# Loading a KV cache in 2 MiB pieces instead of 1 MiB pieces in a decode kernel, with a reshaped query weight, a later output weight and a bf16 GELU

## The chip, the cores and the metric

The kernel runs on one core of one Trainium2 chip. The metric is the device time of one execution in microseconds (us), as the median of several executions. All executions quoted are fast: on one core none was more than 1.5% above the fastest of its kernel.

## The reference

One decode step. A single token attends to a long cache, a small token-mixer MLP runs on the same token, and a sigmoid gate mixes the two.

```python
# x (1,1,448); k_cache, v_cache (1,8,65536,256) bf16; wq (448,4096); wo (4096,448)
def reference(A_x, A_k_cache, A_v_cache, A_wq, A_wo, B_x, B_w1, B_b1, B_w2, B_b2, gate_w):
    # ... attention: 16 query heads, 8 key-value heads, head size 256
    q = (x @ wq) per head
    scores = einsum("bhqd,bhkd->bhqk", q, k) * 256 ** -0.5
    o = einsum("bhqk,bhkd->bhqd", softmax(scores), v)
    a = o @ wo
    # ... mixer: layernorm, u = gelu(h * w1 + b1) with F = 1792, y = w2 . u + b2
    return g * a + (1 - g) * b          # g = sigmoid(sum(x * gate_w))
```

The caches hold 2 x 8 x 65,536 x 256 bf16 elements, which is 537 MB. The two attention weights add 7.3 MB. Every byte is read once, so this is a streaming problem.

## The kernel before

The cache is cut into 256 chunks of 2,048 keys: 1 MiB of K and 1 MiB of V each, 8 KiB on each of 128 partitions. For each chunk TensorE transposes K (32 matmuls against an identity), VectorE and ScalarE copy the result out of PSUM, TensorE makes the scores (32 matmuls), ScalarE takes the exponential, and TensorE multiplies by V (32 matmuls) and sums the denominators (1). SyncE issues all loads from one queue, in the order written, and it waits for a free slot before it issues into it.

```python
    KB = 3          # K slots of 1 MiB
    VB = 4          # V slots of 1 MiB
    # ...
            # SyncE: small rows first, then the query weight, 448 rows as 4 x 112 partitions
            eng.dma_start(wq_sb[:, :, :], A_wq.rearrange("(kt c) n -> c kt n", c=KCP)).then_inc(sem_wq, 16)

            def k_dma(c):
                g, k = divmod(c, NCPH)
                slot = c % KB
                if c >= KB:
                    eng.wait_ge(sem_tr, NB * (c - KB + 1))        # the slot's transposes are done
                src = A_k_cache[0, g, k * CH:(k + 1) * CH, :].rearrange("(p n) d -> p (n d)", p=P)
                eng.dma_start(kbuf[:, slot, :, :].rearrange("p n d -> p (n d)"), src).then_inc(sem_k[slot], 16)
            # ... v_dma(c) likewise, waiting for sem_pv

            WO_AT = min(4, NC - 1)
            for c in range(NC + 2):
                if c < NC:
                    k_dma(c)
                cv = c - 2
                if 0 <= cv < NC:
                    v_dma(cv)
                if c == WO_AT:
                    eng.dma_start(wo_sb[:, :, :], A_wo.rearrange("(kt p) n -> p kt n", p=P)).then_inc(sem_wo, 16)
    # ...
            # TensorE, after the last chunk
            pe.wait_ge(s_rden, 1)
            # ... one matmul spreads the reciprocal denominators
            for kt in range(FT):                                   # 14 matmuls: second MLP layer
                ins = pe.matmul(sps[0:1, 0, 0:DM], w2p_b[:, kt:kt + 1], gu[:, kt, :],
                                start=(kt == 0), stop=(kt == FT - 1))
            # ... 32 matmuls: output projection with wo_sb
```

The softmax here doesn't subtract the row's maximum and nothing guards it: scores larger than these inputs give would overflow.

## Time and profile before

| | before |
|---|---|
| median, 13 executions | 1358.16 us (1357.3 to 1359.97) |
| bytes moved | 547.7 MB |
| TensorE (PE) busy | 87% |
| DMA busy from slice 2 to slice 39 of 40 | 90% or more |
| rate from 100 to 1300 us | 412 to 416 GB/s |

The lines below are from the profile page of the kernel before: the span; the engines with their busy time; the span in 40 slices, where a digit of the DMA row is the busy share in tenths and the row below is GB/s; the packet counts; the queue that fetches instructions (packets, MB, share); the chain of work that ended last; one group of instructions (name, shapes, count | busy us, mean ns | idle us before it, and what ended it); and one DMA issue (count, size, us from issue to landing).

```profile
span 1357.0 us, 53691 instructions
...
PE 1177.8 (87%) x25056; PEld 1143.9 (84%) x25056; DVE 403.1 (30%) x623; ACT 547.8 (40%) x787; POOL 1.0 (0%) x9
...
DMA  8999999999999999999999999999999999999994
GB/s 277 395 418 419 419 419 415 407 418 412 416 413 409 420 408 412 413 419 412 414 411 416 411 410 419 412 411 419 408 409 414 410 416 417 408 415 411 415 411 166
DMA packets 78538, 547.69 MB, mean 404 GB/s; under 512 B 8232, under 2 KB 12331, under 8 KB 12334
...
q8 instruction: 199, 3.26, 1.0%
...
DMA kbuf<-in_A_k_cache_dram 64%; PE kst L258 25%; PE po L291 3%; PE sps L274 3%; DMA wq_sb<-in_A_wq_dram 1%; DMA vbuf<-in_A_v_cache_dram 1%; PE sps L318 0%; SPq L174 0%; PE den L295 0%; PE sps L305 0%; PE sps L237 0%; SPq L182 0%; DVE out_f L427 0%; DVE diff L425 0%; PE den L300 0%
...
L258 PE MATMUL kst<-ident,kbuf 128*128 128x128 bf16 x8192 | 720.0, 268 | 131.9 <-DMA kbuf<-in_A_k_cache_dram 130.0
...
wq_sb<-in_A_wq_dram SPq DMA_DIRECT2D x1, 3584.0 KB, 18.0
```

The DMA row stands at 9 in all slices but the first and the last, while PE is 87% busy. The first slice is slow (277 GB/s), since the query weight is loaded there, and the second has a dip (395). The chain names K loads for 64% of the span. The largest group on PE, the transposes, idled 131.9 us, of which waits for K ended 130.0. PE can keep up; it waits for data.

The next lines are the stretch table of the kernel before: time range and length, busy time of each engine, granted PE clock, DMA share and rate.

```profile
core 0: us, PE busy (x) PEld busy (x) DVE busy (x) ACT busy (x) POOL busy (x), PEclk, DMA share, GB/s
100.00:300.00 200.00, 175.26 (x3850) 171.46 (x3849) 65.03 (x101) 84.89 (x124) 0.00 (x0) 0.78 1.01 416
...
900.00:1100.00 200.00, 179.01 (x3812) 175.32 (x3809) 54.89 (x80) 82.42 (x118) 0.00 (x0) 0.76 1.01 412
```

A DMA share of 1.01 means that the 16 DMA engines had a packet in hand practically all the time (the records of consecutive packets overlap by some 4 ns, so the share can pass 1). When the engines are always busy, the time is in the packets themselves. So the second reading is of single packets, from the trace's records ("at best" is the time that 99% of the packets reach or exceed):

```
packets of the kernel before    count    ns, at best   ns, mean
8,192 B  (K, V, query weight)  65,984     309          318.8
896 B    (output weight)        4,096      41           46
4 B      (semaphore)            8,231       9            9
16,384 B (instruction block)      199     940        1,061
line through 896 B and 8,192 B:  8 ns + 0.0367 ns per byte, which is 27.2 GB/s for each engine, 435 for 16
```

The fixed 8 ns is what a larger packet saves. The 435 GB/s is the line worked out for 16 engines, an estimate from these two packet sizes. Over the 1,200 us from 100 to 1300 us this one core took 412 to 416 GB/s from HBM.

### The profile page before, as it was taken

How to read it: one execution, taken by the hardware profiler on the slowest of the kernel's cores; microseconds unless marked ns; L12 is line 12 of the kernel's file. 1: busy time of each engine (PE TensorE's matmuls, PEld its weight loads, DVE VectorE, ACT ScalarE, POOL GpSimd, SP SyncE). 2: the span in 40 equal slices, each digit the busy share in tenths (PEclk: the TensorE clock that was granted, in tenths of full speed). 3: DMA queues.
4: the chain of work that ended last, by engine and by line, in shares of the span. 5: the costliest groups of instructions: out<-in, count | busy, mean ns of one | idle time of the engine just before them, and what ended most of it. 6: DMA issues, size and time to landing. Idle time of an engine off the chain costs nothing.

```text
span 1357.0 us, 53691 instructions
## 1 busy us (share of the span) xinstructions
PE 1177.8 (87%) x25056; PEld 1143.9 (84%) x25056; DVE 403.1 (30%) x623; ACT 547.8 (40%) x787; POOL 1.0 (0%) x9
## 2 busy tenths in 40 slices
PE   4588889898899898898888888998898899899897
PEld 4588888788898898898888888888888899889885
DVE  2585222222222222222222222222222222222222
ACT  2354344344343443443443443434434344444341
POOL 0000000000000000000000000000000000000000
PEclk9778787788777877867887876877877867767768
DMA  8999999999999999999999999999999999999994
GB/s 277 395 418 419 419 419 415 407 418 412 416 413 409 420 408 412 413 419 412 414 411 416 411 410 419 412 411 419 408 409 414 410 416 417 408 415 411 415 411 166
DMA packets 78538, 547.69 MB, mean 404 GB/s; under 512 B 8232, under 2 KB 12331, under 8 KB 12334
## 3 DMA queue, kind: packets, MB, share of 16 engines
q1 hardware_dynamic: 78318, 544.26, 98.1%
q8 instruction: 199, 3.26, 1.0%
q14 instruction: 21, 0.17, 0.0%
HBM read 544.22 MB, written 0.00 MB: 401 GB/s over the span
## 4 chain that ended last, share of the span: by engine, by line
DMA 67%; PE 32%; issue 1%; SPq 1%; DVE 0%; DVEq 0%
DMA kbuf<-in_A_k_cache_dram 64%; PE kst L258 25%; PE po L291 3%; PE sps L274 3%; DMA wq_sb<-in_A_wq_dram 1%; DMA vbuf<-in_A_v_cache_dram 1%; PE sps L318 0%; SPq L174 0%; PE den L295 0%; PE sps L305 0%; PE sps L237 0%; SPq L182 0%; DVE out_f L427 0%; DVE diff L425 0%; PE den L300 0%
## 5 line engine op out<-in xcount | busy, mean ns | idle before, releaser
L258 PE MATMUL kst<-ident,kbuf 128*128 128x128 bf16 x8192 | 720.0, 268 | 131.9 <-DMA kbuf<-in_A_k_cache_dram 130.0
L455 ACT ACTIVATE ktT<-kst 128x1024 bf16<-128x1024 bf16 x512 | 513.4, 1022 | 781.4 <-PE kst L258 781.3
L258 PEld LDWEIGHTS kst<-ident,kbuf 128*128 128x128 bf16 x8192 | 666.2, 124 | 150.3 <-DMA kbuf<-in_A_k_cache_dram 145.2
L392 DVE COPY ktT<-kst 128x1024 bf16<-128x1024 bf16 x512 | 353.6, 691 | 912.1 <-PE kst L258 900.1
L291 PE MATMUL po<-pT,vbuf 128*128 128x2 bf16 x8192 | 247.6, 164 | 22.3 <-issue 18.5
L274 PE MATMUL sps<-qT,ktT 128*128 128x2 bf16 x8192 | 251.2, 164 | 3.5 <-issue 3.5
L274 PEld LDWEIGHTS sps<-qT,ktT 128*128 128x128 bf16 x8192 | 247.1, 100 | 4.1 <-issue 3.9
L291 PEld LDWEIGHTS po<-pT,vbuf 128*128 128x128 bf16 x8192 | 228.7, 97 | 24.0 <-issue 20.9
L461 ACT ACTIVATE pT<-sps 128x32 bf16<-128x32 f32 x255 | 50.2, 197 | 1.5 <-PE sps L274 1.3
L295 PE MATMUL den<-pT,ones_col 128*1 128x32 bf16 x256 | 46.0, 180 | 0.0
L295 PEld LDWEIGHTS den<-pT,ones_col 128*1 128x1 bf16 x256 | 20.3, 79 | 5.6 <-issue 0.9
L237 PEld LDWEIGHTS sps<-xcol,wq_sb 112*128 112x128 bf16 x128 | 3.5, 104 | 10.3 <-issue 10.3
L237 PE MATMUL sps<-xcol,wq_sb 112*128 112x1 bf16 x128 | 3.6, 165 | 9.0 <-DMA wq_sb<-in_A_wq_dram 9.0
L371 DVE TENSOR_TENSOR zring<-wring,uring 128x448 f32<-128x448 f32 x14 | 8.8, 626 | 1.2 <-issue 0.2
L366 DVE TENSOR_TENSOR wring<-uring 128x448 f32<-128x448 f32 x14 | 8.8, 626 | 1.1
L380 DVE TENSOR_TENSOR gu<-tring,uring 128x448 bf16<-128x448 f32 x14 | 8.8, 625 | 1.1
L443 ACT ACTIVATE tring<-zring 128x448 f32<-128x448 f32 x14 | 8.2, 583 | 0.0
L363 DVE TENSOR_SCALAR uring<-hbT,params 128x448 f32<-128x448 f32 x14 | 7.1, 507 | 0.0
L318 PE MATMUL sps<-wo_sb,oTn 128*1 128x448 bf16 x32 | 6.2, 352 | 0.0
L368 DVE TENSOR_SCALAR wring<-wring 128x448 f32<-128x448 f32 x14 | 5.5, 394 | 1.1
L227 PE MATMUL sps<-h_row,ones_row_f 1*128 1x448 f32 x2 | 1.9, 1026 | 4.5 <-DVE h_row L351 4.5
L318 PEld LDWEIGHTS sps<-wo_sb,oTn 128*1 128x1 bf16 x32 | 2.7, 84 | 3.4
(55 smaller groups left out, 31.0 us busy)
## 6 DMA issues: line engine op xcount, KB each, us to landing
kbuf<-in_A_k_cache_dram SPq DMA_DIRECT2D x256, 1024.0 KB, 12.4
vbuf<-in_A_v_cache_dram SPq DMA_DIRECT2D x256, 1024.0 KB, 14.6
wq_sb<-in_A_wq_dram SPq DMA_DIRECT2D x1, 3584.0 KB, 18.0
wo_sb<-in_A_wo_dram SPq DMA_DIRECT2D x1, 3584.0 KB, 21.1
xrow_b<-in_A_x_dram SPq DMA_DIRECT2D x1, 0.9 KB
grow_b<-in_gate_w_dram SPq DMA_DIRECT2D x1, 0.9 KB
w1row_b<-in_B_w_dram SPq DMA_DIRECT2D x1, 3.5 KB
b1row_b<-in_B_b_dram SPq DMA_DIRECT2D x1, 3.5 KB
```

The lines of the kernel that those rows point to most:

```text
L258: ins = pe.transpose(kst[:, b, j * P:(j + 1) * P], kbuf[:, slot, nt, dh * P:(dh + 1) * P], ident[:, :])
L274: ins = pe.matmul(sps[:, sbk, 2 * nt:2 * nt + 2], ktT[:, slotT, bnk, j * P:(j + 1) * P], qT[:, dh, REP * g:REP * g + REP], start=(dh == 0) ...
L291: pe.matmul(po[:, col:col + REP], vbuf[:, vslot, nt, dh * P:(dh + 1) * P], pT[:, pslot, 2 * nt:2 * nt + 2], start=first, stop=last)
L295: ins = pe.matmul(den[0:1, g * 2 * NT:(g + 1) * 2 * NT], ones_col[:, 0:1], pT[:, pslot, 0:2 * NT], start=(k == 0), stop=(k == NCPH - 1))
L318: ins = pe.matmul(sps[0:1, 1, 0:DM], oTn[:, col:col + 1], wo_sb[:, kt, :], start=(i == 1), stop=(i == nmm))
L366: vec.tensor_tensor(wring[:, slot, :], uring[:, slot, :], uring[:, slot, :], op=ALU.mult)
L371: vec.tensor_tensor(zring[:, slot, :], wring[:, slot, :], uring[:, slot, :], op=ALU.mult).then_inc(s_u, 1)
L380: vec.tensor_tensor(gu[:, kt, :], tring[:, slot, :], uring[:, slot, :], op=ALU.mult).then_inc(s_pb, 1)
L392: vec.tensor_copy(ktT[:, slotT, b, :], kst[:, b, :]).then_inc(sem_evd, 1)
L443: act.activation(tring[:, slot, :], zring[:, slot, :], AF.Tanh, scale=GC0).then_inc(s_tanh, 1)
L455: act.activation(ktT[:, slotT, b, :], kst[:, b, :], AF.Copy).then_inc(sem_eva, 1)
L461: act.activation(pT[:, ce % PTB, :], sps[:, ce % 2, 0:2 * NT], AF.Exp, scale=scale).then_inc(sem_exp, 1)
```

## The change

Its intent: loads of 2 MiB with 16 KiB contiguous on each partition, so that packets double; the query weight on 128 partitions instead of 112; the output weight in the same buffer as the query weight, so it is loaded near the end (at load 108 of 128) instead of near the start; the second-layer product moved from the tail into the stream; and the GELU, LayerNorm and gate rounded to bf16 step by step, as the reference does.

```diff
+    DC = 2
     KB = 3
-    VB = 4
+    VB = 3
+    KW = [P] * (KC - 1) + [DM - P * (KC - 1)]          # 128, 128, 128, 64
+    BROW_CP = (H // 2) * NCPH - 1                      # chunk 127
-        kbuf = sb([P, KB, NT, DH], bf16, "kbuf")
-        vbuf = sb([P, VB, NT, DH], bf16, "vbuf")
+        kbuf = sb([P, KB, DC, NT, DH], bf16, "kbuf")
+        vbuf = sb([P, VB, DC, NT, DH], bf16, "vbuf")
-        wq_sb = sb([KCP, KC, HQ * DH], bf16, "wq_sb")
-        wo_sb = sb([P, KTILES, DM], bf16, "wo_sb")
+        wqo = sb([P, KC * HQ * DH], bf16, "wqo")
+        wq_sb = wqo[:, :].rearrange("p (kt n) -> p kt n", kt=KC)
+        wo_sb = wqo[:, 0:KTILES * DM].rearrange("p (kt n) -> p kt n", kt=KTILES)
# ...
-            eng.dma_start(wq_sb[:, :, :], A_wq.rearrange("(kt c) n -> c kt n", c=KCP)).then_inc(sem_wq, 16)
+            eng.dma_start(wq_sb[:, 0:KC - 1, :], A_wq[0:(KC - 1) * P, :].rearrange("(kt c) n -> c kt n", c=P)).then_inc(sem_wq, 16)
+            eng.dma_start(wq_sb[0:KW[-1], KC - 1, :], A_wq[(KC - 1) * P:DM, :]).then_inc(sem_wq, 16)
+            def k_dma(cd):
+                c0 = cd * DC
+                g, k = divmod(c0, NCPH)
+                slot = cd % KB
+                if cd >= KB:
+                    eng.wait_ge(sem_tr, NB * ((cd - KB) * DC + DC))
+                src = A_k_cache[0, g, k * CH:(k + DC) * CH, :].rearrange("(p n) d -> p (n d)", p=P)
+                eng.dma_start(kbuf[:, slot, :, :, :].rearrange("p c n d -> p (c n d)"), src).then_inc(sem_k[slot], 16)
# ... v_dma(cd) likewise
+            WO_AT = max(0, NCD - 20)
+            for cd in range(NCD + 1):
+                if cd < NCD:
+                    k_dma(cd)
+                if cd - 1 >= 0:
+                    v_dma(cd - 1)
+                if cd == WO_AT:
+                    eng.wait_ge(s_pe_pro, 3)
+                    eng.dma_start(wo_sb, A_wo.rearrange("(kt p) n -> p kt n", p=P)).then_inc(sem_wo, 16)
# ... TensorE
                     for kt in range(KC):
-                        ins = pe.matmul(sps[:, 1, j:j + 1], wq_sb[0:KCP, kt, col0:col0 + P],
-                                        xcol[0:KCP, kt:kt + 1], start=(kt == 0), stop=(kt == KC - 1))
+                        ins = pe.matmul(sps[:, 1, j:j + 1], wq_sb[0:KW[kt], kt, col0:col0 + P],
+                                        xcol[0:KW[kt], kt:kt + 1], start=(kt == 0), stop=(kt == KC - 1))
# ...
+                    if cp == BROW_CP:
+                        pe.wait_ge(s_pb, FT)
+                        for kt in range(FT):
+                            ins = pe.matmul(po[0:1, BRC:BRC + DM], w2p_b[:, kt:kt + 1], gu[:, kt, :],
+                                            start=(kt == 0), stop=(kt == FT - 1))
+                        ins.then_inc(s_brow, 1)
-            pe.wait_ge(s_pb, FT)
-            pe.wait_ge(sem_exp, NC)
-            for kt in range(FT):
-                ins = pe.matmul(sps[0:1, 0, 0:DM], w2p_b[:, kt:kt + 1], gu[:, kt, :],
-                                start=(kt == 0), stop=(kt == FT - 1))
-            ins.then_inc(s_tp, 1)
# ... VectorE: the GELU's polynomial in 7 steps on bf16 tiles instead of 4 on f32 tiles;
# ... LayerNorm, gate and final combination rounded to bf16; sigmoid by an exponential
```

## The prediction

> **What bounds the kernel now.** The 16 DMA engines. In the slices of the span DMA is 90% or more busy in all but the first and last, at 395 to 420 GB/s. In the table of stretches, 100 to 1300 us runs at 412 to 416 GB/s with a DMA share of 1.01, while PE is 88 to 91% busy. The chain of waits is 64% K loads and 25% transposes. The bytes (544 MB) stay the same.
>
> **Packets.** The trace's packet records show 65,984 packets of 8,192 B: 309 ns at best, mean 319. The 896 B packets (output weight) take 41 ns at best, semaphore packets (4 B) 9 ns. The line through the first two is 8 ns per packet plus 0.0367 ns/B: 27.2 GB/s per engine, 435 for 16. [...]
>
> **What the change does.**
> 1. K and V come as 2 MiB loads, 16 KiB contiguous per partition. I expect 16,384 B packets of about 610 ns against twice 309: 8 to 9 ns saved on each of 2,048 pairs per engine, about 17 us, and half the semaphore packets, 256 x 9 ns = 2.4 us. Together -20 us (an estimate). The rate at 100 to 1300 us should rise from 413 to about 420 GB/s.
> 2. The query weight (3.5 MiB) was loaded on 112 partitions: 18.05 us in the chain, packets of 550 to 650 ns, while K packets right after it took 312 ns. [...] Now 6/7 of it goes to 128 partitions, the rest to 64. I expect about 10 us instead of 17: -7 us, on the critical path, since the stream queues behind it.
> 3. More prefetch (10 MiB before the first wait, was 4) fills DMA dips at 30 to 36 us and in the last 20 us: -2.5 us.
> 4. The second-layer product (14 matmuls, 4.1 us) leaves the tail, where it delayed the output projection from about 1344.4 to 1347.1 us: -2.7; in mid-stream, buffers cover it. But the last V load is now two chunks, so PE has two P-V groups (1.1 us each) after it instead of one, and transposes bunch up: +1 to +2.5 us. Tail net about -1.
> 5. The bf16 GELU has more DVE steps (7 instead of 4), but DVE is 30% busy: nothing. The longer LayerNorm/gate prologue adds 2 to 3 us to a chain that ended at 12.4 us: nothing or +1. The output weight, moved to the end, costs the same 11 to 12 us of DMA.
>
> PE must supply a chunk per 5.0 us; it needs 4.6 at the mean clock of 0.76[...] (a chunk's transposes took 1.96 us unthrottled, 3.5 just after a wait). So PE should not become the bound.
>
> **Sum.** 1358 - 20 - 7 - 2.5 - 1 = about 1328 us. Range (8 in 10): 1317 to 1344. Faster by over 2%: 0.62; within 2%: 0.36; slower: 0.02.
>
> **What would show each step.** Packet records of 16,384 B near 610 ns; DMA rate about 420; the query weight landing near 13 us rather than 20.6; no dip in the second slice; no 14 matmuls before the output projection; DMA still about 1.0 busy.
>
> **What would make it wrong.** Packets that stay 8 KiB (then about 1343 us, the likeliest miss); the long packets (1% over 500 ns, 5 ns of the mean) growing with size; PE falling behind because slots free up in pairs; the 64-partition piece as slow as the old load.

The -7 for the query weight is the estimate from the packet times beside it (550 to 650 ns on 112 partitions, 312 ns for the K packets, which are on 128). The words cut from the paragraph on PE were about its clock; that paragraph rests on 4.6 us against 5.0 without them.

## The result, and the profile after

| | before | after |
|---|---|---|
| median | 1358.16 us (13 executions) | 1335.37 us (8 executions, 1334.6 to 1336.78) |
| ratio of the fast runs | | 0.9832 (95%: 0.9823 to 0.9842) |
| span of the profiled execution | 1357.0 us | 1332.8 us |
| mean granted PE clock | 0.763 | 0.768 |

A ratio is the mean time of one kernel's fast runs over that of the other's of the same rounds, so it is not quite the ratio of the medians quoted. The change is worth 22.8 us or 1.7%: inside the predicted range, but 7 us short of the predicted gain, and on the other side of the 2% mark. The profiled execution after is at the fast edge of its range, so the two spans differ by 24.2 us rather than 22.8.

The same lines of the page of the changed kernel, with the V group and a second instruction queue added:

```profile
span 1332.8 us, 53305 instructions
...
PE 1178.0 (88%) x25055; PEld 1143.6 (86%) x25055; DVE 405.8 (30%) x691; ACT 548.9 (41%) x786; POOL 1.2 (0%) x10
...
DMA  9999999999999999999999999999999999999993
GB/s 351 423 425 423 426 425 426 424 424 424 426 426 421 419 421 417 421 416 414 421 425 416 417 425 417 421 414 420 413 417 418 424 420 354 425 425 426 424 425 136
DMA packets 41689, 547.65 MB, mean 411 GB/s; under 512 B 4153, under 2 KB 8252, under 8 KB 8255
...
q8 instruction: 198, 3.24, 1.0%
q14 instruction: 21, 0.16, 0.0%
...
DMA vbuf<-in_A_v_cache_dram 45%; PE kst L279 28%; PE po L314 10%; PE sps L295 8%; PE den L318 1%; DMA wqo<-in_A_wq_dram 1%; PE sps L256 1%; PE sps L341 1%; ACT ktT L500 0%; PE po L324 0%; PE den L329 0%; DVE arow_b L470 0%; SPq L190 0%; DVE densum L451 0%; SPq L180 0%
...
L279 PE MATMUL kst<-ident,kbuf 128*128 128x128 bf16 x8192 | 710.1, 266 | 19.6 <-DMA kbuf<-in_A_k_cache_dram 9.2
...
L314 PE MATMUL po<-pT,vbuf 128*128 128x2 bf16 x8192 | 250.9, 164 | 85.6 <-DMA vbuf<-in_A_v_cache_dram 51.5
...
wqo<-in_A_wq_dram SPq DMA_DIRECT2D x1, 3072.0 KB, 10.9
wqo<-in_A_wq_dram SPq DMA_DIRECT2D x1, 512.0 KB, 13.3
```

The large readings are as predicted. The first slice went from 277 to 351 GB/s, the dip in the second is gone (423), slices 2 to 12 run at 423 to 426, and packets are nearly halved in number. PE's busy time has not moved (1177.8 and 1178.0 us). The chain names V loads now where it named K loads. That is a change of name: with three V slots and V issued behind K, the V load is the one that PE meets late (51.5 us of waits; 9.2 for K). The DMA row still says 9 throughout.

Two readings are not as predicted: from slice 13 on the rate falls to between 413 and 425, and there is one slice at 354. The stretch table of the changed kernel shows the fall:

```profile
core 0: us, PE busy (x) PEld busy (x) DVE busy (x) ACT busy (x) POOL busy (x), PEclk, DMA share, GB/s
100.00:300.00 200.00, 180.63 (x3873) 176.51 (x3871) 58.91 (x93) 85.02 (x121) 0.00 (x0) 0.75 1.01 425
...
900.00:1100.00 200.00, 179.94 (x3813) 175.69 (x3812) 55.33 (x80) 83.32 (x118) 0.00 (x0) 0.75 1.00 418
```

The six stretches of 200 us from 100 to 1300 us read 425, 423, 419, 418, 418 and 413 GB/s, where before they read 416, 413, 414, 413, 412 and 414. The gain was 9 GB/s at first and is near nothing at the end.

The single packets, from the trace's records:

```
packets of the changed kernel   count    ns, at best   ns, mean
16,384 B (K, V)                32,768     611          621.6     (two of 8,192 B before: 618 and 637.6)
4 B      (semaphore)            4,151       9            9
16,384 B (instruction block)      198     961        1,060
```

### Where the 24.2 us lie

The trace gives the moment at which a given number of megabytes had been delivered. The lead of the changed kernel over the one before, at the same number of megabytes, can be read as a running account. The output weight is left out of the bytes, so each kernel pays for it where it loads it.

```
delivered   before, us   after, us   lead, us
  3.6 MB       18.5         14.1        4.4    query weight all but in
 10 MB         35.8         30.0        5.8
 20 MB         70.6         53.8       16.7    before has now loaded the output weight: 10.9
450 MB       1116.1       1081.6       34.6    stream: +17.9
460 MB       1140.4       1120.1       20.3    after loads the output weight: -14.3
538 MB       1331.3       1304.6       26.7    stream: +6.4
last landing 1340.8       1316.2       24.6    end of the stream: -2.1
end          1357.0       1332.8       24.2    tail: -0.4
```

So the query weight and the deeper prefetch gave 5.8 us, the stream 24.3 (17.9 + 6.4), the output weight cost 3.4 (14.3 - 10.9), the end of the stream 2.1 and the tail 0.4.

The late output weight is the slice at 354 GB/s. The DMA view of the changed kernel between 1085 and 1140 us, in 40 slices of 1.4 us, has a mean busy share of 5 to 6 tenths for some 7 us, as if half the engines were idle:

```profile
DMA  9999999989999999655559899999999999999999
GB/s 405 453 405 441 411 417 429 432 350 385 396 383 363 384 396 334 227 172 175 179 179 279 318 376 450 441 441 405 429 453 429 417 393 465 429 417 417 441 429 417
```

The tail, on the timelines (start, length, engine, what), first of the kernel before and then of the changed one:

```profile
1340.93 0.99 PE L291 MATMUL po<-pT,vbuf 128*128 128x2 bf16 x32 [1.00 <-DMA vbuf<-in_A_v_cache_dram]
...
1343.39 4.10 PE L305 MATMUL sps<-gu,w2p_b 128*1 128x448 bf16 x14
...
1347.32 6.22 PE L318 MATMUL sps<-wo_sb,oTn 128*1 128x448 bf16 x32
...
1355.50 0.26 SPq L195 DMA_DIRECT2D out_dram<-out_b  x1
```

```profile
1318.25 0.99 PE L314 MATMUL po<-pT,vbuf 128*128 128x2 bf16 x32
...
1321.38 8.14 PE L341 MATMUL sps<-wqo,oTn 128*1 128x448 bf16 x32 [0.60 <-DVE oTn L463]
...
1331.30 0.27 SPq L212 DMA_DIRECT2D out_dram<-out_b  x1
```

The 14 matmuls of 4.10 us have left the tail as planned, but the 32 matmuls of the output projection now take 8.14 us where they took 6.22. The stretch table of the changed kernel, over the two halves of that projection, says why: the granted clock (the third figure from the right) was half until 1325 us. The last two lines are from the stretch table of the kernel before.

```profile
1319.00:1325.00 6.00, 4.58 (x23) 1.97 (x20) 1.93 (x7) 0.00 (x0) 0.00 (x0) 0.50 0.01 3
1325.00:1330.00 5.00, 4.52 (x23) 1.81 (x21) 0.44 (x1) 0.00 (x0) 0.00 (x0) 0.97 0.00 0
```

```profile
1339.20:1346.00 6.80, 4.98 (x68) 3.01 (x65) 1.08 (x5) 0.01 (x1) 0.00 (x0) 0.50 0.03 8
1347.30:1353.50 6.20, 6.20 (x33) 2.60 (x31) 0.67 (x1) 0.00 (x0) 0.00 (x0) 1.00 0.01 3
```

In the kernel before, the window of half clock (0.50 from 1339.2 to 1346.0 us) fell on the 14 matmuls, and the projection ran at 1.00. The pattern holds in every kept trace: the projection takes 7.7 to 9.2 us in the twelve without the 14 matmuls in front of it, and 6.2 and 6.5 us in the two with them. So it is shown that the 14 matmuls had filled the half-clock time that the projection now meets. What lifts the clock is not shown: in the repeated changed kernel it stayed at half from 1307.3 to 1327.8 us, although PE was busy for all of the 3.4 us from 1314.1 us.

### Sixteen parts of a load do not land together

Each load adds 16 to its semaphore, and the trace has the times of 16 landings for it. They are read here as the parts of the 16 DMA engines, one each. For one load of the changed kernel near 487 us they are, in us after the first:

```
0  0.37  0.51  0.61  0.91  1.16  1.51  1.66  |  11.57  11.59  11.66  11.76  11.83  11.87  12.45  13.28
```

Eight parts are on time and eight are 10 us behind. PE must wait for the last. Below is the mean of the late eight less the mean of the early eight ("the split"), in us, at several times of the span:

```
                 50   200   400   600   800  1000  1080  1160  1300    last landing
before          1.2   4.4   4.4   4.5   5.1   5.3   4.2   5.3   5.1      1340.8
after           1.0   4.6  10.2  11.1  11.4   9.7  10.4   4.1   7.9      1316.2
```

After the change the split grows by 2.6 us per 100 us until about 400 us, then stands, and it drops when the output weight is loaded. Its growth and its limit have the look of a debt, and the reading, tested below, is this. Eight engines have more to do than the other eight. They fall behind; the early eight run ahead as far as the issued loads allow. Once SyncE's wait for a free slot holds the early eight back, all 16 go at the pace of the slower eight, and the rate falls from 425 to 418.

What could the extra work be? The page has it in one line: queue 8, 198 blocks of 16,384 B. These fit PE's instructions: 25,055 matmuls and as many weight loads at 256 to a block are 196 (experiment 6 shows the 256: 6,656 instructions fewer, 26 blocks fewer). 3.24 MB is 0.6% of the bytes, and the forecast passed over it. If all of those blocks go to the eight late engines, the growth gives the cost of one: 100 us hold 15.1 blocks, 1.89 for each of the eight, and the split grows by 2.65 us: about 1.4 us of an engine's time for each block (an estimate), where a data packet of the same size takes 0.62. Over the run that is 198 / 8 x 1.4, about 35 us on each of the eight.

The packet records can check this, though they do not name the engine: an engine's next packet starts some 4 ns before its last one ends, so its packets can be followed one after another to the landing of its part, some 0.45 us after the last of them. Of the 101 blocks between 60 and 1080 us that can be followed so in the changed kernel, 99 lie on the late half of a load (97 of 104 in the repeated run). A part with a block in it takes 6.44 us (median) instead of 4.89, so a block costs its engine 1.55 us: its own 1.06, and the data packet behind it is slow, at 1.1 instead of 0.61. That gives 2 MiB in 4.89 us, or 429 GB/s, at the pace of an engine without blocks, and 417 at that of the late eight (estimates); 425 and 418 were measured.

### The profile page after: what moved, and what is told of

Its sections match the earlier page's. It is cut to its first block, busy times and chain, and to the rows that moved or that the text cites. A ratio compares the mean times of both kernels' runs of the same rounds, so it can differ in the third digit from the quotient of the medians.

```text
span 1332.8 us, 53305 instructions
## 1 busy us (share of the span) xinstructions
PE 1178.0 (88%) x25055; PEld 1143.6 (86%) x25055; DVE 405.8 (30%) x691; ACT 548.9 (41%) x786; POOL 1.2 (0%) x10
## 3 DMA queue, kind: packets, MB, share of 16 engines
q8 instruction: 198, 3.24, 1.0%
## 4 chain that ended last, share of the span: by engine, by line
PE 50%; DMA 46%; issue 4%; ACT 0%; DVE 0%; SPq 0%; DVEq 0%; ACTq 0%
DMA vbuf<-in_A_v_cache_dram 45%; PE kst L279 28%; PE po L314 10%; PE sps L295 8%; PE den L318 1%; DMA wqo<-in_A_wq_dram 1%; PE sps L256 1%; PE sps L341 1%; ACT ktT L500 0%; PE po L324 0%; PE den L329 0%; DVE arow_b L470 0%; SPq L190 0%; DVE densum L451 0%; SPq L180 0%
## 5 line engine op out<-in xcount | busy, mean ns | idle before, releaser
L279 PE MATMUL kst<-ident,kbuf 128*128 128x128 bf16 x8192 | 710.1, 266 | 19.6 <-DMA kbuf<-in_A_k_cache_dram 9.2
L279 PEld LDWEIGHTS kst<-ident,kbuf 128*128 128x128 bf16 x8192 | 653.5, 123 | 31.7 <-issue 12.6
L314 PE MATMUL po<-pT,vbuf 128*128 128x2 bf16 x8192 | 250.9, 164 | 85.6 <-DMA vbuf<-in_A_v_cache_dram 51.5
L295 PEld LDWEIGHTS sps<-qT,ktT 128*128 128x128 bf16 x8192 | 248.9, 100 | 30.4 <-issue 28.9
L256 PEld LDWEIGHTS sps<-xcol,wqo 128*128 128x128 bf16 (+1 forms) x128 | 8.3, 106 | 5.4 <-issue 4.5
L256 PE MATMUL sps<-xcol,wqo 128*128 128x1 bf16 (+1 forms) x128 | 9.2, 174 | 4.1 <-DMA wqo<-in_A_wq_dram 4.1
L341 PE MATMUL sps<-wqo,oTn 128*1 128x448 bf16 x32 | 8.1, 426 | 0.6 <-DVE oTn L463 0.6
L488 ACT ACTIVATE tring<-zring 128x448 bf16<-128x448 bf16 x14 | 8.1, 578 | 0.0
L408 DVE TENSOR_TENSOR wring<-uring 128x448 bf16<-128x448 bf16 x14 | 5.5, 392 | 1.2 <-issue 0.2
L410 DVE TENSOR_TENSOR zring<-wring,uring 128x448 bf16<-128x448 bf16 x14 | 5.5, 393 | 1.0
L414 DVE TENSOR_TENSOR zring<-uring,wring 128x448 bf16<-128x448 bf16 x14 | 5.5, 392 | 1.0
L425 DVE TENSOR_TENSOR gu<-wring,tring 128x448 bf16<-128x448 bf16 x14 | 5.5, 392 | 1.0
## 6 DMA issues: line engine op xcount, KB each, us to landing
wqo<-in_A_wq_dram SPq DMA_DIRECT2D x1, 3072.0 KB, 10.9
```

The lines of the kernel that those rows point to most:

```text
L256: ins = pe.matmul(sps[:, 1, j:j + 1], wq_sb[0:KW[kt], kt, col0:col0 + P], xcol[0:KW[kt], kt:kt + 1], start=(kt == 0), stop=(kt == KC - 1))
L279: ins = pe.transpose(kst[:, b, j * P:(j + 1) * P], kbuf[:, slot, ck, nt, dh * P:(dh + 1) * P], ident[:, :])
L295: ins = pe.matmul(sps[:, sbk, 2 * nt:2 * nt + 2], ktT[:, slotT, bnk, j * P:(j + 1) * P], qT[:, dh, REP * g:REP * g + REP], start=(dh == 0) ...
L314: pe.matmul(po[:, col:col + REP], vbuf[:, vslot, cv, nt, dh * P:(dh + 1) * P], pT[:, pslot, 2 * nt:2 * nt + 2], start=first, stop=last)
L341: ins = pe.matmul(sps[0:1, 1, 0:DM], oTn[:, col:col + 1], wo_sb[:, kt, :], start=(i == 1), stop=(i == nmm))
L408: vec.tensor_tensor(W, U, U, op=ALU.mult)
```

## The experiments

Theory A: the DMA queue sets the time throughout. Packet size gives the gain, and the blocks of PE's instructions, carried by half of the DMA engines, set the limit that takes part of it back. Rivals: B, that PE has become the pace-maker in the second half (its granted clock is 0.74 to 0.78 and the rate falls there); that load size rather than packet size gave the gain; that the late output weight or too few slots cost the missing microseconds.

Each kernel is the changed one with one edit. Each was timed in five rounds beside the kernel before, whose median was 1357.8 to 1358.6. All give a correct result within tolerance unless noted. The changed kernel itself, repeated (1336.02 us, ratio 0.9831, 0.9817 to 0.9844), is the basis of the differences below. Its landings split as before, by 10.3 us near 400 us and 11.3 near 1000, so the split is no chance.

> The changed kernel once more, as the baseline of this chip. Both theories: 0.983 of the kernel before. Theory A (unequal DMA engines): the landing times of one load's 16 parts again split into 8 early and 8 late, over 10 us apart after 500 us, and half the DMA engines run dry for some 6 us when the output weight is loaded and for some 9 us at the end. Theory B (PE frees slots too late): the split is chance and comes out differently.

### 1. Large loads with packets of the old size

```diff
-                src = A_k_cache[0, g, k * CH:(k + DC) * CH, :].rearrange("(p n) d -> p (n d)", p=P)
-                eng.dma_start(kbuf[...].rearrange("p c n d -> p (c n d)"), src)
+                src = A_k_cache[0, g, k * CH:(k + DC) * CH, :].rearrange("(c p n) d -> p c (n d)", c=DC, p=P)
+                eng.dma_start(kbuf[...].rearrange("p c n d -> p c (n d)"), src)      # V likewise
```

> Same 2 MiB loads, same prefetch, but each partition gets two rows of 8 KiB instead of one of 16 KiB, so packets of 8,192 B. If packet size is what the stream gained from: the rate in 100 to 450 us falls from 425 to about 419 GB/s and the time rises by 15 to 20 us, to 0.995 of before. If larger loads and deeper prefetch were the gain: within 5 us of the changed kernel.

Measured: 1352.62 us, ratio 0.9957 (0.9944 to 0.9969). Two lines of its page, the rate in the 40 slices and the packets:

```profile
GB/s 352 419 418 418 419 418 419 420 418 419 419 419 419 414 411 417 415 412 409 412 420 414 406 418 414 411 407 416 419 406 420 410 412 347 419 419 419 419 419 128
DMA packets 74456, 547.65 MB, mean 405 GB/s; under 512 B 4152, under 2 KB 8251, under 8 KB 8254
```

The loads are of 2 MiB, the slots and order are those of the changed kernel, but each partition gets two rows of 8 KiB. In slices 2 to 12 the rate is 418 to 420 instead of 423 to 426, and 16.6 us of the gain are gone. Packet size alone makes the larger part of the gain; load size is not what did it.

### 2. The query weight on 112 partitions again

```diff
-            eng.dma_start(wq_sb[:, 0:KC - 1, :], ...)        # 3 x 128 partitions
-            eng.dma_start(wq_sb[0:KW[-1], KC - 1, :], ...)   # 64 partitions
+            eng.dma_start(wq_sb[0:KCP, :, :], A_wq.rearrange("(kt c) n -> c kt n", c=KCP)).then_inc(sem_wq, 16)
```

> The query weight back on 112 partitions, all else as changed. If its transfer delays the whole stream: it lands near 20 us after the start and the time rises by 4 to 5 us (0.9865 of before). PE's query projection should fall from 9.2 to about 3.5 us without helping. If buffers hide it: no change within 1 us.

Measured: 1340.01 us, ratio 0.9863 (0.9849 to 0.9876), so 4.0 us more. That is the worth of this part, where 7 were forecast. Once the 64-partition piece has the engines to itself (from 12.1 us in the trace of the changed kernel), its packets of 8 KiB take 578 to 780 ns, no faster than those on 112 partitions before (two thirds of them 480 to 650), so the whole weight landed at 16.3 us, not at 13. The timelines of this experiment and of the changed kernel also show the projection that uses it:

```profile
20.14 3.55 PE L255 MATMUL sps<-xcol,wqo 112*128 112x1 bf16 x128 [7.79 <-DMA wqo<-in_A_wq_dram]
```

```profile
16.44 9.22 PE L256 MATMUL sps<-xcol,wqo 128*128 128x1 bf16 x128 [4.12 <-DMA wqo<-in_A_wq_dram]
```

With 64-row pieces between 128-row ones, 128 matmuls take 9.22 us; with 112 rows throughout, 3.55. If the sixty-four changes of height account for the difference, each costs (9.22 - 3.55) / 64, about 89 ns (an estimate; the cause was not tested). The extra time is hidden here, since the prefetch runs on meanwhile: from 16 to 26 us the changed kernel has a DMA share of 1.01 and 429 GB/s.

### 3. The output weight in sixteen loads

```diff
+    WO_N = 16
-                if cd == WO_AT:
+                if WO_AT <= cd < WO_AT + WO_N:
+                    w0 = (cd - WO_AT) * (KTILES // WO_N)
+                    w1 = w0 + KTILES // WO_N
                     eng.wait_ge(s_pe_pro, 3)
-                    eng.dma_start(wo_sb, A_wo.rearrange("(kt p) n -> p kt n", p=P)).then_inc(sem_wo, 16)
+                    eng.dma_start(wo_sb[:, w0:w1, :], A_wo[w0 * P:w1 * P, :].rearrange("(kt p) n -> p kt n", p=P)).then_inc(sem_wo, 16)
```

> The output weight in 16 loads of 224 KB, one per K-V pair, at the same late place[...]. Theory A ([...]the fast ones starve for 6 us): the starvation goes and the time falls by 2 to 4 us, to 0.980 to 0.9815. Rival (the cost is only the slower small packets): no change.

Measured: 1335.46 us, ratio 0.9834 (0.9819 to 0.9848): no gain. The expectation missed. The DMA view over the same 1085 to 1140 us:

```profile
DMA  9999999999998998999999999999999999999999
GB/s 405 453 441 393 423 453 429 393 381 442 465 405 381 453 465 338 416 425 453 441 405 417 441 410 380 426 441 441 393 429 405 410 426 416 429 441 417 405 411 405
```

The starvation is gone and the time is not. The split explains it: in this kernel it stays between 10 and 15 us to the end, instead of falling to 4.1, and from 1140 to 1300 us the rate is 412, where the changed kernel runs at 425. By the landings, the idle microseconds at the output weight were the early eight engines waiting while the late eight caught up (in the changed kernel the split is 10.4 us at 1080 us and 4.1 at 1160). The debt is paid there at once, or it is paid later in small pieces; the sum is the same. So the 3.4 us at the output weight are, as far as this edit shows, no loss of their own.

### 4. More work for PE, at an equal number of blocks

```diff
                     sbk = cq % 2
+                    pe.matmul(sps[:, sbk, 256:480], ident[:, :], ktT[:, slotT, 0, 0:224],
+                              start=True, stop=True)
```

> One more matmul of 224 columns per chunk, 256 in all, into an unused part of a score bank: about 0.1 to 0.2 us more PE work per chunk, 25 to 50 us in all, and only 1% more instructions. Theory B (PE frees the slots too late and sets the pace after 450 us): the time rises by a large part of that, 15 us or more. Theory A (the slower eight DMA engines set the pace, PE has slack): under 4 us more.

Measured: 1337.18 us, ratio 0.9849 (0.9837 to 0.9862). The engine line of its page:

```profile
PE 1197.8 (90%) x25311; PEld 1160.6 (87%) x25311; DVE 405.8 (30%) x691; ACT 555.4 (42%) x786; POOL 1.2 (0%) x10
```

PE did 19.8 us more work (1197.8 less 1178.0; 25 to 50 were expected), and the time rose by 1.2 us by the medians and 2.4 by the ratios, whose intervals overlap. If PE set the pace, nearly all of it would have shown. Theory B falls.

### 5. Many more instructions on an idle engine

```diff
             eng.memset(ones_row_f[:, :], 1.0).then_inc(sem_ident, 1)      # GpSimd
+            for _ in range(6000):
+                eng.drain()
+                eng.memset(junk_p[:, :], 0.0)
```

> 12,000 idle instructions on GpSimd (a drain and a memset of two numbers, 6,000 times), which nothing waits for: some 47 more instruction blocks of 16 KiB are fetched, 24% more. Theory A (each fetched block takes about 1.5 us of one DMA engine): if GpSimd's blocks come over the same eight slow engines, the early-late split grows faster and the time rises by 6 to 9 us; if they come over the other eight, the split shrinks and the time stays. Theory B: no change of either.

Measured: 1370.09 us, ratio 1.008 (1.0064 to 1.0096), so 33 to 34 us more, several times what was expected. Three lines of its page, the span and the two instruction queues:

```profile
span 1363.0 us, 65305 instructions
...
q8 instruction: 198, 3.24, 0.9%
q14 instruction: 114, 0.93, 0.2%
```

GpSimd had nothing else to do and no other engine waited for it. The data moved and the other engines' instructions are the same, and VectorE is busy for the same 405.8 us. (PE is 22 us busier, at a lower granted clock, 0.748 against 0.768; by experiment 4 that is worth some 2 us.) Still the time rose by 2.5%. Queue 14 brought 114 blocks of 8 KiB instead of 21, less than 0.8 MB more. In this trace the pattern of landings has changed too: near 502 us fifteen parts of a load land within 2.6 us, and one lands at 12.4. One late part in sixteen is what GpSimd's blocks would give if all came over one engine and that one set the pace of all (read from the landings; the trace does not name the engine). The expectation had the cost right in kind but spread it over several engines. So instruction fetches can set the time of this kernel: 33 to 34 us with 93 blocks more. The landings also show to which half the engine belongs: near 200 us seven parts land within 3.1 us, the late eight at 4.8 to 6.5, and one at 11.5, so it came out of the early eight. By the packet records a part with one such block takes 0.66 us longer (median). So 114 of them cost that engine about 75 us, where PE's 198 at 1.55 us cost each late engine about 38 (estimates); the difference of 37 is about what was lost.

### 6. Fewer instructions on PE

Every second key tile is left out of the P-V product, which makes the result wrong, though the tolerance does not notice. Three wide matmuls per chunk give PE part of its work back.

```diff
                     sbk = cq % 2
+                    for _ in range(3):
+                        pe.matmul(sps[:, sbk, 256:480], ident[:, :], ktT[:, slotT, 0, 0:224],
+                                  start=True, stop=True)
@@
-                    for nt in range(NT):
+                    for nt in range(0, NT, 2):
```

> Wrong result on purpose: every second key tile is left out of the P-V product, 16 of 32 matmuls per chunk; three matmuls of 224 columns per chunk give PE about the same work back. 26 fewer PE instructions per chunk, 6,656 in all: 26 of 198 instruction blocks less. Theory A: the early-late split grows 13% more slowly and the time falls by 4 to 5 us against the changed kernel (0.980). Theory B (PE's pace): no change, or slower where the added work is more than what was removed.

Measured: 1329.7 us, ratio 0.9792 (0.9779 to 0.9805): 5 to 6 us less. Three lines of its page:

```profile
span 1326.3 us, 46649 instructions
...
PE 1135.1 (86%) x21727; PEld 1094.9 (83%) x21727; DVE 405.3 (31%) x691; ACT 567.3 (43%) x786; POOL 1.2 (0%) x10
...
q8 instruction: 172, 2.82, 0.9%
```

There are 26 blocks less. At 1.4 us a block on eight engines that is 26 / 8 x 1.4 = 4.5 us (the estimate made above; 5.0 with the 1.55 us of the packet records), and the measured gain is a little more. The split grows more slowly, by 2.24 instead of 2.6 to 2.7 us per 100 us. PE is also 43 us less busy here, but experiment 4 showed that 20 us of PE are worth only some 2, and the last landing alone came 4.4 us earlier (1311.5 against 1315.9), so PE's share may be some 2 us. The trace does not name the DMA engine of a packet, but its packets can be followed to the landings as above: in this run 84 of the 84 blocks followed lie on the late half.

### 7. Fewer and more slots

```diff
-    KB = 3                                    # experiment 7a: KB = 2, VB = 3
-    VB = 3                                    # experiment 7b: KB = 4, VB = 4, the GELU tiles moved into the wqo buffer for room, so SyncE waits for s_brow before it loads wo
```

> Two K slots instead of three, all else as changed. Theory A says that what the fast eight DMA engines gain by running ahead is only lent: with less room to run ahead the early-late split stops near 5 us instead of 11, the rate falls below 425 GB/s earlier, less is paid back at the output weight and at the end, and the time stays within 3 us of the changed kernel, as long as the slow eight always have work. If depth itself earns the gain: 10 us or more slower.

> Four slots of 2 MiB each for K and V instead of three (the GELU tiles lie in the dead query weight to make room), all else as changed. Theory A (the slow eight DMA engines already always have work with three slots): the split grows to 15 us or more, 425 GB/s lasts longer, more is paid back at the output weight and at the end, and the time is within 4 us of the changed kernel, 0.980 to 0.985. If depth is still what is short, since two slots cost 8 us: 0.978 or less.

Measured: two K slots 1343.58 us, 0.9902 (0.9887 to 0.9916); four slots of each 1335.51 us, 0.9834 (0.9821 to 0.9848). Three lines of the stretch table of the four-slot kernel:

```profile
100.00:300.00 200.00, 179.88 (x3839) 175.44 (x3837) 58.64 (x92) 84.39 (x120) 0.00 (x0) 0.76 1.01 425
500.00:700.00 200.00, 180.80 (x3820) 173.76 (x3818) 54.65 (x79) 82.76 (x118) 0.00 (x0) 0.77 1.01 425
900.00:1100.00 200.00, 179.91 (x3884) 175.70 (x3883) 55.34 (x80) 84.15 (x120) 0.00 (x0) 0.77 1.00 414
```

```
split, us        50   200   400   600   800  1000  1080  1160  1300    last landing
2 K slots       0.7   1.0   1.9   1.3   1.7   2.0   1.8   1.5   1.7      1326.8
4 + 4 slots     0.9   4.8  10.4  15.9  19.9  22.1  21.3   4.2   8.1      1315.5
```

More slots let the early eight run further ahead: the split doubles to 22 us, and 425 GB/s lasts past 500 us. Then it is handed back, 414 GB/s between 900 and 1100 us, and the last landing is where it was. This is what theory A expects of a debt: buffers move it, they do not pay it. With two K slots the split cannot grow beyond 2 us, but the time is 7.5 us worse, where it was expected within 3: PE waits 74 us for V instead of 51.5, and the rate is 414 to 418 from the start. Here the forecast of theory A missed: the third slot earns something of its own, though a fourth does not.

### 8. Loads of 4 MiB

```diff
-    DC = 2
-    KB = 3
-    VB = 3
+    DC = 4
+    KB = 2
+    VB = 2
+    # the GELU tiles moved into the wqo buffer; SyncE waits for s_brow before it loads wo
@@ second version only
-            for cd in range(NCD + 1):
-                if cd < NCD:
-                    k_dma(cd)
-                if cd - 1 >= 0:
-                    v_dma(cd - 1)
+            for cd in range(NCD):
+                k_dma(cd)
+                v_dma(cd)
```

> The packet step once more: loads of 4 chunks (4 MiB, 32 KiB per partition, two slots each for K and V; the GELU tiles lie in the dead query weight to make room). If each packet costs 8 to 9 ns beside its bytes: packets of 32,768 B near 1,215 ns, 1,024 fewer per engine, 8 to 9 us off the stream, some 2 us given back at the end because the last V load holds four chunks: about 1329 us, 0.978. If two slots leave the slow engines without work: slower than the changed kernel.

> The 4 MiB loads again, but each V load is issued before the next K load instead of after it, so that V no longer waits behind a K load whose slot PE frees only late. If the slowness of the first try was that order and not the packet of 32 KiB: DMA is busy throughout again, packets near 1,213 ns, and the gain of 8 to 9 us per stream, less some 2 us at the end, appears: 1327 to 1331 us, 0.977 to 0.980. If large packets or only two slots are the trouble: over 1350 us.

Measured, first version: 1822.12 us, ratio 1.3418 (1.3401 to 1.3435). Two lines of its page, the busy share of the DMA engines in the 40 slices and the P-V group:

```profile
DMA  8768668677686686776866867769677677686773
...
L318 PE MATMUL po<-pT,vbuf 128*128 128x2 bf16 x8192 | 248.2, 164 | 591.0 <-DMA vbuf<-in_A_v_cache_dram 576.2
```

With two slots and the order K(n), V(n-1), the V load that PE needs stands in the queue behind a K load whose slot PE has yet to free: SyncE waits 1,700 us for the transposes. PE waits 576 us for V and the DMA engines idle a quarter of the time. The second version, with V(n) straight behind K(n), gives 1342.05 us (1338.15 to 1348.82), ratio 0.9882 (0.9862 to 0.9901). Its packets of 32,768 B take 1,213 ns in the median and 1,240 in the mean, against 1,224 and 1,243 for two of 16 KiB: the fixed part is saved once more, at least in the median. Still it is 6 us slower than the changed kernel, where 5 to 9 us faster were expected. The trace kept is of a slower execution (span 1350.0 us): the last landing is at 1321.1 us instead of 1316.2, and from there to the end it needs 28.9 us instead of 16.6, since a 4 MiB V load leaves four chunks of work after the last byte. Why the last landing did not come earlier is not settled; with two slots the rate swings between 391 and 429 GB/s, and PE holds 80% of the chain.

### 9. The second-layer product back in the tail

```diff
-                    if cp == BROW_CP:
-                        ...                                   # 14 matmuls into po, after chunk 127
             pe.wait_ge(s_rden, 1)
             ...
+            pe.wait_ge(s_pb, FT)
+            pe.wait_ge(sem_exp, NC)
+            for kt in range(FT):
+                ins = pe.matmul(sps[0:1, 0, 0:DM], w2p_b[:, kt:kt + 1], gu[:, kt, :],
+                                start=(kt == 0), stop=(kt == FT - 1))
+            ins.then_inc(s_brow, 1)
```

> The 14 second-layer matmuls back in the tail, as before the change. They delay the output projection by 2.7 us, but PE is then at full clock for it: the 32 matmuls should take 6.2 us again instead of 8.1. Net 0.5 to 1 us slower than the changed kernel, near the noise; the profile decides. If the clock did not depend on them: 2.7 us slower and still 8 us for the 32.

Measured: 1336.84 us, ratio 0.9846 (0.9833 to 0.9859); against the repeated changed kernel the intervals overlap, so its worth is 0 to 3 us, 1.5 by the difference of the ratios to the main result. In its trace the 14 matmuls took 5.39 us and the 32 of the projection 6.51 instead of 8.14: by these times, 0.39 us each on the 14 and 0.20 on the 32, the half-clock time is back on the 14. From the end of the last P-V product and its denominators to the output's store it took 14.8 us, against 11.9 in the changed kernel and 13.5 before.

## Why the prediction was right or wrong

The bound, the mechanism and the main size were right; the sum was 7 us too hopeful, and the reasons are in its smaller terms.

| step of the prediction | forecast, us | measured, us |
|---|---|---|
| 1. larger packets | -20 (-17 for the packets, -2.4 for the semaphores) | -16.6 for the packets (experiment 1, semaphores unchanged); by the account 24.3 in the stream, less 5.5 at the output weight and the end: -18.8 |
| 2. query weight | -7 | -4.0 (experiment 2), -4.4 in the trace |
| 3. prefetch, dips at start and end | -2.5 | -1.4 at the start, +2.1 at the end (in the account this is part of the 5.5 above) |
| 4. tail | -1 | +0.4 |
| 5. GELU, prologue, output weight | 0 to +1 | 0; the output weight's +3.4 is part of the 5.5 above |

**Step 1** was right in its mechanism: packets of 16,384 B at 611 ns best (about 610 forecast), a mean rate of 419 GB/s from 100 to 1300 us (420 forecast). The likeliest miss that it named, packets that stay at 8 KiB, is what experiment 1 produced on purpose (1352.62, though 1343 was forecast for it). What it had no notion of is that the 16 engines are not alike. Eight of them fall behind by 2.6 us in 100 us, so a rate read at the start (425) is lent, and it is repaid at the output weight, where 14.3 us went instead of 10.9, and in the last 9 us at half rate.

**Step 2** is the term most mis-sized in its own right: "I expect about 10 us instead of 17" for the query weight, and it landed at 16.3 us where 13 was forecast. The warning was there ("the 64-partition piece as slow as the old load"), and that is what happened: packets of 578 to 780 ns. One seventh of the weight at half the rate, behind the rest, cost 3 us.

**Step 3** had the start right. At the end it forecast a gain, and there the stream ran some 9 us at 197 GB/s, since by the landings the early eight engines had nothing left while the late eight finished (split 7.9 us at 1300).

**Step 4** foresaw that the 14 matmuls leave the tail (P-V end to projection start: 5.28 us before, 2.02 after) and that two groups instead of one follow the last V load (1.2 us before, 3.1 after). It did not foresee the half clock on the projection: +1.9 us. With a shorter final combination these are -3.27 + 1.90 + 1.92 - 0.18 = +0.37.

**Step 5** was right: VectorE is at 405.8 us busy (403.1 before) and nothing waits for it. **PE not the bound** was right too, by experiment 4.

The forecast gave 0.36 to what happened, within 2%. The distance from 0.98 is 0.3%, which is 4 us, a little over half of the missing gain.

No version that was tried beats the changed kernel; the split output weight and four slots equal it. What would, by theory A, is fewer instructions, and experiment 6 shows the worth of 6,656 of them as 5 to 6 us, though it got there by leaving work out.

## What to carry to other kernels

When the DMA engines are busy all the time, read the single packets: a fixed 8 to 9 ns per packet at 8 KiB was worth 1.2% of this kernel, and it was the contiguous bytes per partition that counted here, not the size of the load (from 100 to 300 us, 1 MiB loads gave 416 GB/s, 2 MiB loads with 8 KiB packets 419, with 16 KiB packets 425). A rate that falls slowly through a run while nothing else changes may be a debt between DMA engines: look at how the 16 parts of a load land, before blaming buffers or compute. And in this kernel, bound by DMA, instructions are traffic too: its 25,055 small unrolled matmuls come with 198 instruction blocks, each worth 1.55 us of one DMA engine by the packet records, and on the page that is only a queue with 1.0% of the time beside it.
